# A gated scan and a cosine layer in one kernel: the queries' transposition, the squares of the logs, the split weights, the guards and the verdict change places

## The chip, the cores and the metric

The kernel runs on one core of a Trainium2 chip. The metric is the device time of one execution in microseconds (us). A core has TensorE (PE; its weight loads are listed as PEld), VectorE (DVE), ScalarE (ACT), GpSimd (POOL) and SyncE (SP). Each has an instruction queue of its own that runs in order; what stands behind a waiting instruction waits too. Transfers are issued by SP, POOL or ACT and carried out by 16 DMA engines that all of them share.

## What is computed

```python
# gateloop, q, k, v, a_re, a_im: (4, 8, 768, 48)
mag = np.sqrt(a_re * a_re + a_im * a_im)
scale = np.minimum(mag, 0.999) / (mag + 1e-06)
a_re_n, a_im_n = (a_re * scale, a_im * scale)
for t in range(S):
    new_re, new_im = ar * S_re - ai * S_im, ar * S_im + ai * S_re
    S_re, S_im = new_re + k_t v_t^T, new_im
    y[:, :, t] = q_t S_re
# act_gcu on x = y as (3072, 384); w_in (384, 2048), w_out (2048, 384)
h = x @ w_in
return ((h * np.cos(h)) @ w_out).astype(np.float32)
```

The weights arrive as doubles: the program reads them as 64-bit words and makes floats of them.

## The kernel before

**Groups and stages.** The 3072 rows are 24 chunks of 128 steps; two chunks make a group, so there are 12 groups. The recurrence is done in closed form: running sums of the logarithms of the decay (`lgs`, one matmul by a triangle of ones) and of its phase (`phs`), powers `P` and `Q` of them, then keys and queries multiplied by powers and by cosine and sine (`ks`, `qs`, made in `g_stack`), scores `sc` of chunk against chunk, masked into `atm`, and outputs `yp`. These go through DRAM into `xT`, the input of the cosine layer.

Groups 0 and 1 run in an order written out by hand. From group 2 on a loop `for n in range(2, NG)` builds one stage for each n. Stage n does, in this order on PE: the scores and outputs of group n (`chunks`) and, between them, the second product (`products`: `sum` and `op`) of group n-1; `lgs` and `phs` of group n+1; and the first product (`first`, tiles `hp`) of group n in eight parts `jp` of 256 columns. The scores of the next stage follow directly on the last `hp`.

**Who sets the order.** `weave` sorts the steps of a stage by the places given as fractions and emits them. PE's order is fixed by that (`chain`), as are the table functions of ACT (`special`, with the squares of the logs) and POOL's transfers. On DVE and the rest of ACT a planner orders the instructions when the program is built, by its own estimate of the times: of those that it takes to be ready, the one emitted first goes first. `behind(a, b)` makes it put a after b on the same engine, with no wait on the chip. SP and DVE run then in the order so found.

**Keys and queries.** `f_transpose` (lines 932 to 952) turns `ks` and then `qs` on DVE (tile `tr`), writes the result to DRAM (`moved`), and reads it back as `kT` (four transfers) and `qT` (one), all on SP. The turn of the queries of group n+1 stands behind `X[n]["gated"]`, the first gate product of group n.

**Gates.** For each jp, ACT computes the sine of `hp` (the cosine, by a shifted phase) into `gate` and the square of `hp` for the check of its range (`junk`); DVE multiplies (`gate<-hp,gate`). `hp` has three places in PSUM, so a jp can start when the gate three before it is done.

**Three halves.** For jp 4 to 7 and from a certain group on (`FROM`), the product is made of three products of rounded halves: of the weights (`wh`, `wl`, `wx`, made once by `three_halves`: three passes on DVE, two on ACT) and of x (`xh`, `xl`, `xx`, made in every group by `x_halves`). The crossed product `hb` comes out on ACT (`cross_out`) and is added on DVE (`whole_sum`, rows `hp<-hp,gate`) behind the gate product of the jp before, so for these jp sine, square, product and sum of two neighbours take turns.

**Logs.** `log_steps` starts with two squares on ACT (`lg<-re`, `tan<-im`) and their sum, then logarithms and exponentials (another table of ACT), and splits the sum's argument `lg` into `hi` (ACT) and `lo` (DVE) for PE. In before these squares are emitted at the beginning of a stage, behind the last gate of the stage before.

**Guards.** From stage 4 on, two 768 KB pieces of the original weights are read again in every stage by POOL (`raw`), cut on DVE and checked on ACT (`guard`). They wait on POOL for the last gate of the stage before (`wait_for`). `raw` has the same single buffer (`tr`) as the turned keys, and in before the halves of the weights had it too.

**The tail.** After the loop: the seven products of the last group, for which the gates are mixed on DVE (`mixed`: `s<-gate`; `mixed_again`: `gate<-gate`, `gate<-s,gate`), and the `verdict`, small reductions of the checks whose result chooses between this output and a general path.

Of the kernel before, what the change touches and what calls it, by code (L numbers as in the profile page):

```python
# [487 lines left out]
def fast_path(ctx, tc, q, k, v, a_re, a_im, moe_w_in, moe_w_out, out, least, odd, wide,  # L488
# [158 lines left out]
    def guard(src):  # L647

        _, e = fetched(src)
        vector.tensor_scalar(out=e, in0=e, scalar1=1, scalar2=21,  # L650
                             op0=ALU.logical_shift_left, op1=ALU.logical_shift_right)
        scalar.activation(out=e.bitcast(F32), in_=e, func=AF.Relu, scale=-1.0, bias=least_e_b,
                          accum_out=odd[:, ds(next(odds), 1)])
# [80 lines left out]
    def log_steps(g, i, n):  # L734
# [40 lines left out]
        vector.tensor_tensor(out=mag, in0=mag, in1=sq, op=ALU.mult)  # L775
        if lower:
            lower()
# [154 lines left out]
    def f_transpose(g, i, n, name):  # L932


        if i == 0:
            X[g][name] = ft.tile([D2, G * H, Q4, 32] if name == "kT" else [D2, Q4, G * H, 32], F32,
                                 tag=name, name=name, bufs=1)
        pool, tag = (ft, "tr") if name == "kT" else (gt, "pair")
        tr = pool.tile([C, NB, n * H, 32], F32, tag=tag, name="tr", bufs=1)
        turn = vector.transpose(out=tr, in_=X[g][name[0] + "s"][:, ds(i * H, n * H)].rearrange(  # L940
            "p x a d -> p x (a d)").rearrange("p x (r b) -> p b x r", b=NB))
        X[g][name + " turn"] = turn
        if name == "qT" and "gated" in X[g - 1]:
            behind(turn, X[g - 1]["gated"])
        moved = rows_d.tile([Q4, D2, n * H, 32], F32, tag="moved", name="moved", bufs=3)
        nc.sync.dma_start(out=moved.rearrange("q (r b) x j -> (q r) b x j", b=NB), in_=tr)
        if name == "kT":
            for q4 in range(Q4):
                nc.sync.dma_start(out=X[g][name][:, ds(i * H, n * H), q4], in_=moved[q4])
# [21 lines left out]
    def f_scores(n, hh):  # L971
# [5 lines left out]
        for h in range(HH):  # L977
# [4 lines left out]
            out=y["atm"][:, ts(hh, HH)], in0=ps, in1=causal.unsqueeze(1).to_broadcast([C, HH, C]), op=ALU.mult)  # L982

# [111 lines left out]
    def halves(g):  # L1095

        if g == PLAIN:
            for name in "wl", "wx":
                right[name] = stage["pool"].tile([C, len(THREE), ND, 256], F32R, name=name)
        for n, jp in enumerate(THREE):  # L1100
            if FROM[jp] == g:
                yield from three_halves(jp, right["wl"][:, n], right["wx"][:, n])

    def three_halves(jp, wl, wx):

        cut_ = ft.tile([C, ND, 256], F32, tag="tr", name="cut", bufs=1)
# [3 lines left out]
        yield  # L1110
        vector.tensor_tensor(out=wl, in0=w, in1=cut_, op=ALU.subtract)
        w_in[jp] = wts.tile([C, ND, 256], F32R, tag=f"w_in{jp}", name="wh", bufs=1)
        scalar.copy(out=w_in[jp], in_=cut_)
        yield
        vector.scalar_tensor_tensor(out=wx, in0=wl.bitcast(F32), scalar=-SHIFT, in1=cut_,
                                    op0=ALU.mult, op1=ALU.add)
        scalar.mul(out=wl, in_=wl.bitcast(F32), mul=SHIFT)

    def x_halves(g):
# [14 lines left out]
        def lower():  # L1134
            scalar.copy(out=x["xh"], in_=x["cut"])
            low = vector.tensor_tensor(out=x["xl"], in0=all_of(), in1=x["cut"], op=ALU.subtract)
            if g + 1 < NG:
                behind(low, X[g + 1]["qT turn"])

        def apart():  # L1140
            vector.scalar_tensor_tensor(out=x["xx"], in0=x["xl"].bitcast(F32), scalar=-SHIFT,
                                        in1=x["cut"], op0=ALU.mult, op1=ALU.add)
# [6 lines left out]
    def mm1_three(g, jp, ps):  # L1149
# [27 lines left out]
        for part in (straight, crossed) if k == 0 else (crossed, straight):  # L1177
            part()
# [8 lines left out]
    def whole_sum(g, jp):  # L1187
        ps = X[g]["hp"][jp]
        behind(vector.tensor_tensor(out=ps, in0=ps, in1=X[g]["gate"][jp], op=ALU.add),
               X[g]["product"])  # L1190

    def gate_sine(g, jp):
# [6 lines left out]
        scalar.activation(out=junk, in_=ps, func=AF.Square, scale=size,  # L1199
                          accum_out=wide[:, ds(g * (NJ // 2) + jp, 1)])  # L1200

    def gate_product(g, jp):
# [8 lines left out]
        x.setdefault("gated", gated)  # L1211
# [32 lines left out]
    FROM, UPPER, SHIFT = {4: 2, 5: 3, 6: 3, 7: 4}, 0xFFFFF000, 4096.0  # L1244
# [23 lines left out]
    def mixed(g, p):  # L1268
# [4 lines left out]
        vector.tensor_tensor(out=s1, in0=a21, in1=a22, op=ALU.add)  # L1273
# [73 lines left out]
    def stepwise(part, count):  # L1347

        part = iter(part)
        return [lambda: next(part, None) for _ in range(count)]  # L1350

# [57 lines left out]
    def first(g):  # L1409
        return [lambda jp=jp: mm1(g, jp) for jp in range(NJ // 2)]  # L1410
# [8 lines left out]
    def guarded(g, count):  # L1419
# [3 lines left out]
        for _ in range(min(count, len(guards))):  # L1423
            yield lambda: guard(guards.pop(0))
# [281 lines left out]
    for n in range(2, NG):  # L1706
        turned_keys, plain = list(keys(n + 1)), n == PLAIN
        split = x_halves(n)
        if n + 1 < NG:
# [7 lines left out]
              (stepwise(halves(n), 3 * list(FROM.values()).count(n)), 0.1, 0.5),  # L1717
# [4 lines left out]
              (mixes(n, 0, 2), 0.92, 1.0), (guarded(n - 1, per) if n > 3 else [], 0.1, 0.56))  # L1722
# [6 lines left out]
    weave((mixes(NG - 1, 2, 4), 0.0, 0.1), ([judged], 0.05, 0.15),  # L1729
# [95 lines left out]
```

## Time and profile before

| | |
|---|---|
| runs | 676.52, 671.46, 675.76 us; median 675.76 |
| profiled execution | 675.03 us, its span 673.2 us |
| PE busy | 635.2 us, 94% |
| DVE busy | 534.6 us, 79% |
| ACT busy | 433.5 us, 64% |
| POOL busy | 30.7 us, 5% |
| DMA | 94.95 MB, mean 141 GB/s |

The profile records one execution: for each instruction its start, its duration and what ended the idle time before it. The span runs from the first instruction to the last. A row of the timeline names the start, the duration, the engine, the line, the operation, its tiles as output<-inputs, and in brackets the idle time of the engine before it with what ended that. Most rows carry the line of a helper (L678 for DVE and ACT, L689 for PE), so the tiles' names tell them apart. PEclk is the share of TensorE's full clock that was granted.

### The profile page before, as it was taken

What the parts mean: (1) busy time and instruction counts of PE and PEld (TensorE: products, weight loads), DVE (VectorE), ACT (ScalarE), POOL (GpSimd) and SP (SyncE); (2) the same over time, 40 slices, a digit from 0 to 9 for tenths busy, and PEclk for the clock granted to TensorE, in tenths of its full rate; (3) what the DMA queues carried; (4) which work ended last, traced back from release to release, by engine and by line L of the source; (5) the groups of instructions that cost most, each with busy time, mean ns of one, the idle gap of its engine ahead of it and who ended that gap; (6) DMA issues with size and microseconds to landing.
All of it is one profiled execution on the core that took longest, in us unless ns stands there. A gap on an engine that the chain in (4) does not pass through costs nothing. (4 is left out here: it accounts for less than half of the span.)

```text
span 673.2 us, 11371 instructions
## 1 busy us (share of the span) xinstructions
PE 635.2 (94%) x4291; PEld 573.7 (85%) x4291; DVE 534.6 (79%) x867; ACT 433.5 (64%) x790; POOL 30.7 (5%) x53
## 2 busy tenths in 40 slices
PE   8999999998999999899889999989989999999996
PEld 5888777766899898889889989988989988999995
DVE  6999999887897797797678788788879779864371
ACT  7898786465675693694676587577577578553340
POOL 4011100000000000010000000000000000000000
PEclk9999999999999999999989999989999999999999
DMA  9967846437527638638626836745764763354001
GB/s 244 245 186 171 271 117 168 103 83 185 108 48 188 142 94 212 165 105 182 181 64 159 203 98 158 201 112 124 206 136 110 190 135 114 100 136 141 23 1 31
DMA packets 232924, 94.95 MB, mean 141 GB/s; under 512 B 208701, under 2 KB 221246, under 8 KB 232858
## 3 DMA queue, kind: packets, MB, share of 16 engines
q1 hardware_dynamic: 225320, 68.51, 44.2%
q0 software_dynamic: 5824, 25.50, 11.5%
q8 instruction: 36, 0.59, 0.4%
q10 hardware_dynamic: 1714, 0.11, 0.2%
q14 instruction: 30, 0.25, 0.1%
HBM read 69.28 MB, written 24.81 MB: 140 GB/s over the span
## 5 line engine op out<-in xcount | busy, mean ns | idle before, releaser
L689 PE MATMUL hp<-xT,w_in 128*128 128x256 f32 (+1 forms) x744 | 160.3, 373 | 4.4 <-DVE gate L678 2.4
L689 PEld LDWEIGHTS hp<-xT,w_in 128*128 128x128 f32 x744 | 137.1, 190 | 25.0 <-DMA xT<-x 2.9
L689 PE MATMUL op<-w_out,gate 128*128 128x192 f32 (+1 forms) x464 | 103.6, 373 | 0.8 <-DVE gate L678 0.8
L709 ACT ACTIVATE gate<-hp,half_pi_b 128x512 f32<-128x512 f32 x96 | 66.0, 687 | 54.0 <-PE hp L689 29.2
L689 PEld LDWEIGHTS op<-w_out,gate 128*128 128x128 f32 x464 | 78.5, 190 | 18.2 <-issue 2.2
L678 DVE TENSOR_TENSOR gate<-hp,gate 128x512 f32<-128x512 f32 x60 | 40.9, 685 | 31.5 <-ACT junk L678 31.3
L689 PE MATMUL sc<-qT,kT 96*128 96x128 f32 x384 | 50.7, 281 | 11.6 <-DMA qT<-moved 10.1
L689 PEld LDWEIGHTS sc<-qT,kT 96*128 96x128 f32 x384 | 48.3, 196 | 14.5 <-issue 9.7
L689 PE MATMUL sum<-w_out,gate 128*128 128x192 f32 x304 | 56.9, 337 | 0.0
L678 ACT ACTIVATE junk<-hp 128x512 bf16<-128x512 f32 x96 | 56.8, 592 | 0.0
L689 PEld LDWEIGHTS sum<-w_out,gate 128*128 128x128 f32 x304 | 51.1, 196 | 0.0
L678 DVE SCALAR_TENSOR_TENSOR gate<-hp,gate 128x512 f32<-128x512 f32 x36 | 24.8, 690 | 24.0 <-ACT junk L678 24.0
L678 ACT ACTIVATE ot<-sum 128x192 f32<-128x192 f32 x39 | 12.7, 327 | 46.7 <-PE sum L689 46.5
L689 PE MATMUL hp<-xh,wh 128*128 128x256 f32 x216 | 38.5, 287 | 1.5 <-DVE gate L678 1.5
L678 DVE TENSOR_TENSOR atm<-sc,causal 128x512 f32<-128x512 f32 x48 | 32.5, 685 | 7.3 <-PE sc L689 7.3
L689 PE MATMUL hp<-xl,wl 128*128 128x256 f32 x216 | 37.3, 281 | 0.0
L689 PEld LDWEIGHTS hp<-xh,wh 128*128 128x128 f32 x216 | 30.9, 189 | 4.5 <-DVE gate L678 4.4
L678 DVE TENSOR_TENSOR gate<-gate 128x256 f32<-128x256 f32 x80 | 32.7, 419 | 2.3 <-PE op L689 1.4
L689 PE MATMUL yp<-atm,v 128*48 128x128 f32 x352 | 33.5, 277 | 0.0
L678 DVE TENSOR_TENSOR hp<-hp,gate 128x512 f32<-128x512 f32 x36 | 24.9, 693 | 9.1 <-ACT gate L678 9.1
L705 ACT ACT_TABLE_LOAD x24 | 30.8, 1283 | 1.2 <-PEq L1809 0.7
L689 PEld LDWEIGHTS hp<-xl,wl 128*128 128x128 f32 x216 | 30.6, 188 | 0.0
(163 smaller groups left out, 1248.9 us busy)
## 6 DMA issues: line engine op xcount, KB each, us to landing
moved<-tr SPq DMA_DIRECT2D x20, 768.0 KB
raw<-in_moe_w_in_dram POOLq DMA_DIRECT2D x16, 768.0 KB, 5.2
raw<-in_moe_w_out_dram POOLq DMA_DIRECT2D x16, 768.0 KB, 4.7
kT<-moved SPq DMA_DIRECT2D x40, 192.0 KB
qT<-moved SPq DMA_DIRECT2D x10, 768.0 KB
k<-in_k_dram SPq DMA_DIRECT2D x24, 192.0 KB
q<-in_q_dram SPq DMA_DIRECT2D x24, 192.0 KB
v<-in_v_dram SPq DMA_DIRECT2D x24, 192.0 KB
```

The source lines that it names most:

```text
L678: ins = getattr(self.engine, op)(**kw)
L689: chain(nc.tensor.matmul(out, **kw), "tensor")
L705: chain(nc.scalar.preload_act_table_set(table))
L709: chain(nc.scalar.activation(func=func, **kw))
```

## The change

- The queries' turn is no longer put behind the first gate product of the group; the copy `xh` is put behind the square of the gate emitted last, and `xl` and `xx` behind its product.
- `mm1` gets a flag for the last jp of a group. At that place the first step of the logs of group g+2 (two squares, their sum) is emitted, ahead of the last gate's sine. The sum of halves waits with its gate as `held` instead of looking at jp - 1.
- In the logs, `lo` is made before the product `pair<-pair,tan` and not behind it.
- The masked scores are put behind the last sum of halves of the group before.
- `FROM` goes from {4: 2, 5: 3, 6: 3, 7: 4} to {4: 3, 5: 3, 6: 4, 7: 4}. The halves of the weights are made in stage 2 (jp 4, 5) and stage 3 (jp 6, 7), at places 0.7 and 0.76, when that group has used the plain weights: `first` takes these jp first. Their buffer is that of `yT`.
- The guards' places go from three between 0.1 and 0.56 to 0.1 (the wait), 0.22 (the first) and 0.93 (the second, whose cut on DVE is put behind the gate product of its place).
- In the tail the verdict's first part is emitted first, then all four mixes of the last group, put behind its last gate product; before, two of the four stood in the stage's end.

```diff
-    def guard(src):
+    def guard(src, other=None):
...
+        if other is not None:
+            behind(ins, other)
@@ log_steps
-        vector.tensor_tensor(out=mag, in0=mag, in1=sq, op=ALU.mult)
         if lower:
-            lower()
+            X[g]["low"] = lower()
+        product = vector.tensor_tensor(out=mag, in0=mag, in1=sq, op=ALU.mult)
+        if lower:
+            behind(product, X[g]["low"])
@@ f_transpose
-        if name == "qT" and "gated" in X[g - 1]:
-            behind(turn, X[g - 1]["gated"])
@@ f_scores
+        if "whole" in X[n // G - 1]:
+            behind(y["masked"], X[n // G - 1]["whole"])
@@ halves of one jp (was a generator in three steps)
-        cut_ = ft.tile([C, ND, 256], F32, tag="tr", name="cut", bufs=1)
+        cut_ = ft.tile([C, ND, 256], F32, tag="yT", name="cut", bufs=1)
@@ x_halves
-            scalar.copy(out=x["xh"], in_=x["cut"])
+            behind(scalar.copy(out=x["xh"], in_=x["cut"]), x["square"])
...
+            behind(low, x["product"])
...
+            behind(vector.scalar_tensor_tensor(
+                out=x["xx"], in0=x["xl"].bitcast(F32), scalar=-SHIFT,
+                in1=x["cut"], op0=ALU.mult, op1=ALU.add), x["product"])
@@ mm1
-    def mm1(g, jp):
+    def mm1(g, jp, last):
+
         mm1_sums(g, jp)
         if three(g, jp):
             cross_out(g, jp)
-            if three(g, jp - 1):
-                mm1_gate(g, jp - 1)
+            if "held" in X[g]:
+                mm1_gate(g, X[g]["held"])
+            X[g]["held"] = jp
             whole_sum(g, jp)
-        if not three(g, jp) or jp == NJ // 2 - 1 or not three(g, jp + 1):
+        else:
             mm1_gate(g, jp)
+        if last:
+            if g + 2 < NG:
+                X[g + 2]["steps"] = log_steps(g + 2, 0, G)
+                next(X[g + 2]["steps"])
+            if "held" in X[g]:
+                mm1_gate(g, X[g]["held"])
@@
-    FROM, UPPER, SHIFT = {4: 2, 5: 3, 6: 3, 7: 4}, 0xFFFFF000, 4096.0
+    FROM, UPPER, SHIFT = {4: 3, 5: 3, 6: 4, 7: 4}, 0xFFFFF000, 4096.0
@@ mixed
+        if g == NG - 1:
+            behind(first_, X[g]["product"])
@@ first
-        return [lambda jp=jp: mm1(g, jp) for jp in range(NJ // 2)]
+        late_ = [jp for jp in THREE if FROM[jp] == g + 1]
+        order = late_ + [jp for jp in range(NJ // 2) if jp not in late_]
+        return [lambda jp=jp: mm1(g, jp, jp == order[-1]) for jp in order]
@@ guarded
-            yield lambda: guard(guards.pop(0))
+            yield lambda: guard(guards.pop(0), X[g + 1].get("product"))
@@ the loop
-              (stepwise(halves(n), 3 * list(FROM.values()).count(n)), 0.1, 0.5),
+              (convert[0:1], 0.7, 0.7), (convert[1:2], 0.76, 0.76),
...
-              (mixes(n, 0, 2), 0.92, 1.0), (guarded(n - 1, per) if n > 3 else [], 0.1, 0.56))
+              (mixes(n, 0, 2 * (n < NG - 1)), 0.98 if convert else 0.92, 1.0), (guard_[0:1], 0.1, 0.1),
+              (guard_[1:2], 0.22, 0.22), (guard_[2:3], 0.93, 0.93))
@@ the tail
-    weave((mixes(NG - 1, 2, 4), 0.0, 0.1), ([judged], 0.05, 0.15),
+    weave(([judged], 0.0, 0.0), (mixes(NG - 1, 0, 4), 0.01, 0.1),
```

More of the change, by code (lines that the diff above doesn't have):

```diff
@@ L1707, in fast_path @@
         turned_keys, plain = list(keys(n + 1)), n == PLAIN
-        split = x_halves(n)
-        if n + 1 < NG:
+        split = x_halves(n) if any(three(n, jp) for jp in THREE) else ()
+        guard_ = list(guarded(n - 1, per)) if n > 3 else []
+        convert = [lambda jp=jp: halves(jp) for jp in THREE if FROM[jp] == n + 1]
+        if FROM[THREE[0]] <= n < NG - 1:
             X[n + 1]["upper"] = split[0]
```

38 lines of the change are left out of this document (14 added, 24 removed).

## The prediction

> **What bounds the kernel now.** The page's engine line first, then the list of who made PE wait, over the whole span, cut to the entries that matter here.
>
> ```profile
> PE 635.2 (94%) x4291; PEld 573.7 (85%) x4291; DVE 534.6 (79%) x867; ACT 433.5 (64%) x790; POOL 30.7 (5%) x53
> ```
> ```profile
> PE sc L689 <- DMA qT<-moved: 10.1, 5, 3.2
> PE lgs L689 <- DVE lo L678: 7.3, 8, 1.4
> PE hp L689 <- DVE gate L678: 4.0, 5, 1.4
> PE hp L689 <- DMA xT<-x: 2.0, 2, 1.6
> ...
> PE sc L689 <- issue: 1.3, 1, 1.3
> ```
> PE is the bound, in one fixed order, so an edit is worth what it takes from PE's work or from these waits (total, times, longest), 24.7 us. Two kinds come back in nearly every stage: scores on the queries' transfer (11.4 in six, with the 1.3 put down to "issue" at the same place) and log sums on their lower halves.
>
> Some waits cost again. Three windows of 24 or 25 matmuls, each from the scores that ended such a wait; the clock is the third number from the end:
>
> ```profile
> 338.10:342.95 4.85, 4.85 (x24) 4.85 (x25) 2.54 (x6) 3.84 (x6) 0.74 (x2) 0.65 0.00 0
> ...
> 443.63:448.45 4.82, 4.82 (x25) 4.82 (x25) 3.87 (x8) 3.46 (x6) 1.04 (x2) 0.65 0.01 3
> 497.37:500.53 3.16, 3.16 (x24) 3.16 (x25) 3.16 (x8) 2.06 (x5) 0.00 (x0) 1.00 0.03 5
> ```
> ```profile
> 443.63 1.13 PE L689 MATMUL sc<-qT,kT 96*128 96x128 f32 x8 [1.72 <-DMA qT<-moved]
> ```
> ```profile
> 497.37 1.13 PE L689 MATMUL sc<-qT,kT 96*128 96x128 f32 x8 [1.95 <-DMA qT<-moved]
> ```
> Granted clock 0.65 instead of 1.00 and 4.85 or 4.82 us instead of 3.16: 1.7 us lost, twice, 3.4 in all: after the wait of 3.2 and after 1.72, not after 1.95.
>
> Now the queries' chain in stage 8, whose first product starts at 476.11; times from there are called T. DVE, ACT and SP:
>
> ```profile
> 479.55 0.56 DVE L678 TENSOR_SCALAR cut<-xT 128x768 uint32<-128x768 uint32 x1
> 482.22 0.69 DVE L678 TENSOR_TENSOR gate<-hp,gate 128x512 f32<-128x512 f32 x1 [2.12 <-ACT junk L678]
> 482.83 2.26 DVE L678 STREAM_TRANSPOSE tr<-qs 128x1536 f32<-128x1536 f32 x1
> ```
> ```profile
> 480.19 0.83 ACT L678 CAST xh<-cut 128x768 fp32r<-128x768 f32 x1 [3.55 <-DVE cut L678]
> ```
> ```profile
> 485.12 0.33 SPq L946 DMA_DIRECT2D moved<-tr  x1
> 485.54 4.70 SPq L949 DMA_DIRECT2D kT<-moved  x4
> ```
> The queries turn from T 6.7 to 9.0 only because the first gate stands ahead of them, and that is late because ACT waits 3.55 us with the copy xh ahead of the gate's sine. SP issues in order, so the four kT transfers, ready before, wait for the queries' store too. What the DMA engines do meanwhile (the last two numbers, share and GB/s):
>
> ```profile
> 482.10:485.50 3.40, 3.40 (x18) 2.99 (x17) 3.28 (x3) 2.51 (x7) 0.00 (x0) 1.00 0.01 2
> 485.50:496.10 10.60, 9.92 (x78) 9.29 (x76) 7.60 (x14) 6.41 (x14) 0.00 (x0) 1.00 0.99 222
> ```
> After the keys' store 3.4 us of nothing, then 10.6 us at 0.99, and 1.3 more until PE starts at 497.37. From the queries' store on, the engines are full.
>
> **The change part by part.**
>
> *Queries turned behind the keys.* With the edge gone and xh behind the square, the queries' turn can follow the cut (479.55 and 0.56: T 4.0) and end near T 6.2; if the planner lets the first gate go first, now ready near T 4 as well (matmuls to T 2.6, then sine and square), near T 6.9. I take 6.2: the store leaves 2.8 us earlier. By itself that brings the scores from T 21.3 to 18.5, ahead of PE, which is there at 495.42 (497.37 less 1.95), T 19.3: all 11.4 us gone. The first gate comes no later than now.
>
> *The second guard.* At 0.93 it stands behind the turned keys in the one buffer tr, and nothing else on POOL holds it, the wait for the last gate being long past. So its fetch starts when the keys' store has landed, near T 6 to 7, together with the queries' store. First a row in which a fetch leaves as soon as that buffer is free, then the share of POOL's queue in the window of one fetch (501.0 to 506.1), then both queues in a window (14.0 to 19.5) where such fetches met SP's small packets:
>
> ```profile
> 511.55 0.72 POOL L631 DMA_DIRECT2D raw<-in_moe_w_out_dram  x1 [9.59 <-ACT raw L678]
> ```
> ```profile
> q0 software_dynamic: 144, 0.79, 43.9%
> ```
> ```profile
> q0 software_dynamic: 555, 2.07, 94.7%
> q1 hardware_dynamic: 435, 0.12, 9.1%
> ```
> 43.9% of 5.1 us is 2.24 us of all 16 engines. Where they met, POOL's queue kept 94.7% and SP's 9.1%. So the fetch goes through nearly unhindered, and the queries' chain loses between 0 (should the fetch fall into a hole) and 2.24 us; I take 2.2, the rows of the meeting being the nearest. Scores at T 20.7, PE's wait about 1.4, and this also at the end of stage 10, which has no wait now: 7 x 1.4 = 9.8 for 11.4, **-1.6**. Of six waits now two cost half the clock; of seven, each shorter than 1.72, I take one: **-1.7** of 3.4, between -3.4 (none) and +8.5 (all seven).
>
> The Trainium skill, "TensorE: Matmul & The Clock Gate", Part 1 (What's actually happening), lets the clock fall after an idle window of about 3.4 us. Here it fell after 1.72 us, so the rows decide; by the page none of the new waits would cost clock, and this term would be -3.4.
>
> *Squares ahead of the last sine, lo ahead of pair.*
>
> ```profile
> 498.47 0.69 ACT L709 ACTIVATE gate<-hp,half_pi_b 128x512 f32<-128x512 f32 x1 [1.43 <-DVE hp L678]
> ...
> 499.62 0.84 ACT L753 ACTIVATE lg<-re 128x768 f32<-128x768 f32 x1
> 500.35 0.84 ACT L753 ACTIVATE tan<-im 128x768 f32<-128x768 f32 x1
> ```
> ```profile
> 510.17 1.00 ACT L678 ACTIVATE raw<-raw,least_e_b 128x768 f32<-128x768 uint32 x1
> ```
> ```profile
> 509.62 0.95 DVE L678 TENSOR_TENSOR pair<-pair,tan 128x768 f32<-128x768 f32 x1
> 510.49 0.95 DVE L678 SCALAR_TENSOR_TENSOR lo<-lg,hi 128x768 fp32r<-128x768 f32 x1
> ```
> ```profile
> 511.50 0.45 PE L689 MATMUL lgs<-lo,exact 128*128 128x384 f32 x1 [0.96 <-DVE lo L678]
> ```
> ```profile
> PE lgs L689 <- DVE lo L678: 5.1, 6, 1.2
> ```
> The two squares, 0.73 us apart, fit into the 1.43 us that ACT waits ahead of the last sine; what follows on ACT comes 1.46 us earlier. lo gains 0.87 more (509.62 to 510.49). Against it stands the second guard's check, 1.0 us on ACT, now behind the gate of jp 5, where sines and sums take turns: if it falls between, the last sine is that much later. Net 1.3 to 2.3 us for a wait of 0.96, of which the shorter wait for queries, 0.55, takes back a part. The last row is the list of waits from 209 us on; of its 5.1 I leave 0.3: **-4.8**. Without the cover of the queries' wait PE would come 1.4 us sooner and wait here for what is missing. The two earlier waits, 7.3 less 5.1, lie in groups 2 and 4; lo moves by 0.87 in both, the squares in the second alone: **-1.6** of 2.2.
>
> *Guards and halves out of the second products.* In stage 4 now:
>
> ```profile
> 258.14 0.56 DVE L678 TENSOR_SCALAR raw<-raw 128x768 uint32<-128x768 uint32 x1 [2.10 <-DMA raw<-in_moe_w_in_dram]
> ```
> DVE stands 2.1 us for the second fetch, in the middle of the phases, and the fetch shares the engines with the transfer of xT: of the waits on xT the longest, **-1.6**, goes. Of the 4.0 for gates, all in stages 2 to 4, jp behind three halves are the longest; in stages 2 and 3 the plain jp now come first, but halves of 2.35 us each on DVE (0.56 and twice 0.95, less overlap) come among the gates. **-1.0**, between -4.0 and +2 for a gate held up by one such set.
>
> *FROM.* Two jp, one in stage 2 and one in stage 3, become plain again.
>
> ```profile
> 476.11 10.52 PE L689 MATMUL hp<-xT,w_in 128*128 128x256 f32 x48
> ...
> 489.55 0.51 PE L689 MATMUL hp<-xh,wh 128*128 128x256 f32 x3
> ...
> 491.69 0.52 PE L689 MATMUL hp<-xh,wh 128*128 128x256 f32 x3
> ```
> A plain jp takes 10.52 / 4 = 2.63 us; of three halves one starts 2.14 after the other. 2 x 0.49 = **+1.0**.
>
> *The tail.* All mixes of the last group now stand behind its last gate product.
>
> ```profile
> 650.67 1.10 DVE L678 TENSOR_TENSOR gate<-gate 128x256 f32<-128x256 f32 x3
> ...
> 652.02 0.68 DVE L678 SCALAR_TENSOR_TENSOR gate<-hp,gate 128x512 f32<-128x512 f32 x1
> 652.62 0.24 DVE L1762 TENSOR_REDUCE most<-wide 128x1 f32<-128x96 f32 x1
> ```
> ```profile
> 652.76 0.92 PE L689 MATMUL op<-w_out,gate 128*128 128x192 f32 x4 [0.82 <-DVE gate L678]
> 653.51 0.65 PE L689 MATMUL sum<-t_s,gate 128*128 128x192 f32 x3
> ```
> Without mixes ahead of it the last gate can come up to 0.4 us earlier (the mix ahead of it goes) and end at 652.2. Then come about 0.5 of verdict (the reduction and small ones) and, at 0.34 each (three took 1.10), four sums, four differences and the one that the third product reads first: 652.2 + 0.5 + 9 x 0.34 = 655.8, where PE now starts at 653.51. **+2.3**; +3.3 with the last guard's check in between, nothing if the planner still mixes earlier.
>
> Sum: -1.6 -1.7 -4.8 -1.6 -1.6 -1.0 +1.0 +2.3 = -9.0: the span goes from 673.2 to 664.2, and with the 1.8 us around it the execution from 675.03 to 666.0. The median of the runs, 675.76, is 0.7 above that execution: **667**.
>
> **The rivals.**
>
> *The fetch hides.* If it falls into holes of the chain, no score waits. For it: 482.10 to 485.50 shows the engines empty just there. Against it: with the turn moved that hole closes to under 1 us. Then the log sums bind: PE wants lo 1.95 us before 510.54, T 32.5; lo ends at 511.44 less 1.3 to 2.3, T 33.0 to 34.0. Per stage 1.4 is saved and 0.5 to 1.5 paid, say 0.5 seven times, and 1.7 of clock: **662**.
>
> *Each wait costs the clock.* If all seven waits of 1.4 bring the 1.7 us that 1.72 brought, 10.2 more: **677**, no change. For it 443.63, against it 497.37 and three more of the six.
>
> *The fetch in front, the turn not earlier: slower.* If the planner keeps the turn behind gates and it still ends at T 9.0, the fetch, issued at T 6 to 7, is wholly ahead of the queries' store: scores at T 23.5, a wait of 4.2, seven times 2.8 more than forecast, and the clock as after 3.2 us, six times 1.7 more: 667 + 19.6 + 10.2 = **697**. It decides from a turn that ends past about T 7.5, where 1.3 us in seven stages eat the gain. Against it: of what DVE has, only the first gate is ready about as early.
>
> **How the numbers follow.** The forecast (661 to 671) has 0.5, the hidden fetch (656 to 662) 0.17, the clock, or a gain given back in log sums or tail (671 to 677), 0.22, the slower case 0.11. The range, 656 to 677, holds all but the last and some edges. One per cent, 6.8 us, is about what a measurement of this kernel can tell from no change. Under 669 lie the hidden fetch and most of the forecast: 0.6; within one per cent 0.29; slower 0.11.
>
> **What would show it.** The queries' turn right behind the cut, near T 4; xh no longer ahead of the first sine; the second raw fetch at T 6 to 7, between the two stores, and sc <- qT near 1.4 in seven stages, the tenth included; lgs <- lo under 0.3; the squares ahead of the last sine; in the tail 2 to 3 us of PE ahead of sum<-t_s. The prediction is wrong if the scores' wait is gone or over 2 us, or if gates hold hp up for several us in stages 2 and 3.

## The result, and the profile after

The changed kernel takes 670.45 us (median of 20 runs, 665.73 to 676.51) where the kernel before takes 673.75 beside it (20 runs): a ratio of 0.9934, with a 95% interval of 0.9907 to 0.9961. The ratios of this document leave out the one run of the changed kernel that counts as slow (676.51) and are not the quotients of the medians. That is a gain of 0.4 to 0.9 per cent, within the one per cent that the prediction called no change, though the interval shuts out none at all. The profiled execution took 670.13 us, its span 668.2: 5.0 less than the 673.2 before, where the forecast had 9.0 less.

The engine line of the page, then the list of who made PE wait over the whole span (total, times, longest), of the changed kernel:

```profile
PE 634.7 (95%) x4279; PEld 575.4 (86%) x4279; DVE 528.7 (79%) x862; ACT 432.9 (65%) x787; POOL 31.2 (5%) x53
```
```profile
PE sc L691 <- DMA qT<-moved: 7.8, 6, 3.0
PE hp L691 <- DVE gate L680: 5.1, 1, 5.1
PE sum L691 <- DVE gate L680: 2.5, 1, 2.5
PE sc L691 <- issue: 2.5, 2, 2.3
PE lgs L691 <- DVE lo L680: 2.2, 3, 1.1
```

Scores on the queries' transfer now wait 10.3 us (7.8 and 2.5) for 11.4 before, log sums on their lower halves 2.2 for 7.3. The waits for gates were 4.0 us in five pieces; now they are one piece of 5.1, and the tail has a new one of 2.5. Where these two fall is seen in a table by stage. The first two rows are the kernel before (its stage 2, that is the third group's, and its last stage with the tail), the next two the same stretches of the changed kernel; the first number after the stretch is its length, the third from the end the granted clock:

```profile
155.49:209.06 53.57, 51.08 (x336) 46.91 (x337) 46.23 (x72) 34.88 (x63) 0.00 (x0) 1.00 0.52 118
...
628.11:673.16 45.05, 37.74 (x234) 35.73 (x232) 16.01 (x38) 13.94 (x33) 0.00 (x0) 0.97 0.06 16
```
```profile
155.78:213.24 57.46, 52.32 (x331) 48.13 (x331) 45.01 (x69) 34.75 (x62) 0.00 (x0) 0.97 0.49 112
...
620.54:668.17 47.63, 39.76 (x234) 37.40 (x232) 18.37 (x43) 15.65 (x36) 0.00 (x0) 0.96 0.05 15
```

Stage 2 became 3.9 us longer and the tail 2.6. The stages between them became shorter by 11.8 in all (from 209.06 to 628.11, 419.05 us, against 213.24 to 620.54, 407.30), each of them but stage 10, which became 0.5 longer. The start of stage 2 moved by 0.3. The terms of the prediction that fall between (scores, clock, log sums from 209 us on, xT) come to 9.7, and 2.2 us of waits for gates in stages 3 and 4 are gone beside them. So what was to gain there did gain; the part on gates, which was to gain 1.0, lost more in stage 2 than these 2.2.

What made stage 2 longer is on ACT and DVE, ahead of PE's wait of 5.14 us (three fences of the changed kernel's timeline: start, duration, and in brackets the idle time before and who ended it):

```profile
159.07 2.25 DVE L680 STREAM_TRANSPOSE tr<-ks 128x1536 f32<-128x1536 f32 x1
...
161.28 2.23 DVE L680 STREAM_TRANSPOSE tr<-qs 128x1536 f32<-128x1536 f32 x1
...
165.07 0.96 DVE L680 SCALAR_TENSOR_TENSOR wx<-wl,cut 128x768 fp32r<-128x768 f32 x1
168.16 0.69 DVE L680 TENSOR_TENSOR gate<-hp,gate 128x512 f32<-128x512 f32 x1 [2.12 <-ACT junk L680]
```
```profile
166.12 0.84 ACT L680 ACTIVATE wl<-wl 128x768 fp32r<-128x768 f32 x1 [8.83 <-DVE wx L680]
166.87 0.67 ACT L711 ACTIVATE gate<-hp,half_pi_b 128x512 f32<-128x512 f32 x1
```
```profile
168.90 0.71 PE L691 MATMUL hp<-xT,w_in 128*128 128x256 f32 x1 [5.14 <-DVE gate L680]
```

ACT stood 8.83 us with a pass over the weights' halves at the head of its order, waiting for wx, which DVE reached only behind both transposes of the next group. The first sine of the stage was behind it (an experiment below shows it ready at T 2.9, with T counted from the stage's first product). So the first gate's product came at 168.16, T 12.4, and PE, which had filled its places, waited for it. The clock fell with the wait:

```profile
168.90:172.90 4.00, 4.00 (x11) 3.23 (x12) 3.06 (x4) 3.38 (x7) 0.00 (x0) 0.57 1.04 222
```

At 0.57 over 4.00 us, some 1.7 us more are lost behind it.

Stage 8 of the changed kernel, with T counted from its first product at 469.27, shows the queries' chain in its new form. DVE, POOL, SP and PE:

```profile
472.55 2.25 DVE L680 STREAM_TRANSPOSE tr<-qs 128x1536 f32<-128x1536 f32 x1
474.72 0.52 DVE L680 TENSOR_SCALAR cut<-xT 128x768 uint32<-128x768 uint32 x1
```
```profile
476.36 0.72 POOL L631 DMA_DIRECT2D raw<-in_moe_w_out_dram  x1 [32.88 <-ACT xh L680]
```
```profile
475.84 8.64 SPq L951 DMA_DIRECT2D kT<-moved  x4
484.59 0.86 SPq L953 DMA_DIRECT2D qT<-moved  x1
```
```profile
491.38 0.35 PE L691 MATMUL sc<-qT,kT 96*128 96x128 f32 x1 [3.04 <-DMA qT<-moved]
```

The queries turn from T 3.3 to 5.5, ahead of the cut and of the first gate; they ended at T 9.0 before. The second guard's fetch leaves at T 7.1, as forecast. SP needs 8.64 us to issue the four kT transfers, 4.70 before, and qT goes out only at T 15.3, where it went out at T 14.2 before. In this stage the earlier turn has won nothing, and its scores wait longest, 3.04 us. In five of the seven stages from stage 4 on, kT takes 6.27 to 6.93 us, qT leaves at T 13.2 to 14.0, and a part of the gain is left.

### The profile page after: what moved, and what is told of

Same layout as the page of the kernel before. It is cut to its first block, busy times and chain, and to the rows that moved or that the text cites. A ratio compares the mean times of both kernels' runs of the same rounds, so it can differ in the third digit from the quotient of the medians.

```text
span 668.2 us, 11342 instructions
## 1 busy us (share of the span) xinstructions
PE 634.7 (95%) x4279; PEld 575.4 (86%) x4279; DVE 528.7 (79%) x862; ACT 432.9 (65%) x787; POOL 31.2 (5%) x53
## 3 DMA queue, kind: packets, MB, share of 16 engines
q0 software_dynamic: 5824, 25.50, 11.4%
## 4 chain that ended last, share of the span: by engine, by line
PE 70%; ACT 9%; DVE 8%; DMA 7%; issue 4%; SPq 1%; ACTq 0%; POOL 0%; POOLq 0%; DVEq 0%
PE hp L691 23%; PE op L691 14%; PE sum L691 14%; PE yp L691 5%; PE sc L691 4%; PE sp L691 3%; DMA qT<-moved 3%; PE phs L691 2%; PE hb L691 2%; ACT junk L680 2%; DVE hp L680 1%; ACT gate L711 1%; DMA xT<-x 1%; DVE gate L680 1%; PE lgs L691 1%
## 5 line engine op out<-in xcount | busy, mean ns | idle before, releaser
L691 PE MATMUL hp<-xT,w_in 128*128 128x256 f32 (+1 forms) x768 | 166.5, 376 | 7.1 <-DVE gate L680 5.1
L691 PEld LDWEIGHTS hp<-xT,w_in 128*128 128x128 f32 x768 | 143.0, 192 | 28.1 <-DVE gate L680 5.5
L680 DVE TENSOR_TENSOR gate<-hp,gate 128x512 f32<-128x512 f32 x62 | 42.5, 685 | 37.3 <-ACT junk L680 37.0
L691 PE MATMUL sum<-w_out,gate 128*128 128x192 f32 x304 | 54.6, 328 | 0.0
L691 PEld LDWEIGHTS sum<-w_out,gate 128*128 128x128 f32 x304 | 49.2, 190 | 0.0
L691 PE MATMUL hp<-xh,wh 128*128 128x256 f32 x204 | 37.0, 290 | 0.0
L691 PE MATMUL hp<-xl,wl 128*128 128x256 f32 x204 | 35.2, 281 | 0.0
L691 PE MATMUL sum<-t_s,gate 128*128 128x192 f32 x160 | 31.7, 352 | 2.5 <-DVE gate L680 2.5
L691 PEld LDWEIGHTS sum<-t_s,gate 128*128 128x128 f32 x160 | 27.4, 201 | 5.4 <-issue 4.4
L691 PE MATMUL yp<-qT,state 96*48 96x128 f32 x304 | 30.4, 278 | 0.0
```

Of the source, the lines that this page charges most:

```text
L680: ins = getattr(self.engine, op)(**kw)
L691: chain(nc.tensor.matmul(out, **kw), "tensor")
```

## The experiments

Each kernel of the table has its ratio to runs of the kernel before on the same chip.

| kernel | median us | ratio to before (95%) | profiled span |
|---|---|---|---|
| changed kernel | 670.45 | 0.9934 (0.9907 to 0.9961) | 668.2 |
| halves behind the gates | 662.39 | 0.9827 (0.9767 to 0.9887) | 662.9 |
| mixes early | 668.14 | 0.9915 (0.9883 to 0.9947) | 666.2 |
| second guard held back | 675.84 | 1.0049 (1.0020 to 1.0078) | 673.7 |
| turn behind the gate again | 682.95 | 1.0169 (1.0078 to 1.0260) | 682.9 |
| squares back | 693.16 | 1.0281 (1.0236 to 1.0326) | 692.4 |
| lo back | 667.06 | 0.9865 (0.9820 to 0.9911) | 669.2 |
| halves behind the gates, no second guard | 653.72 | 0.9704 (0.9666 to 0.9743) | 651.3 |
| halves behind the gates, mixes early | 660.97 | 0.9796 (0.9766 to 0.9825) | 659.6 |
| the same, guard among second products | 654.34 | 0.9692 (0.9652 to 0.9732) | 649.8 |
| before, log part alone | 665.44 | 0.9839 (0.9790 to 0.9889) | 663.8 |
| before, queries' part alone | 670.41 | 0.9951 (0.9909 to 0.9993) | 668.1 |

The kernel before took 674.14, 674.77 and 673.96 us in the three sets.

**Halves behind the gates.** The theory was that the place of the halves, and nothing else in the first gates, costs stage 2 its time.

```diff
 def halves(jp):
-    vector.tensor_scalar(out=cut_..., in0=w..., scalar1=UPPER, ...)
+    x = X[FROM[jp] - 1]
+    behind(vector.tensor_scalar(out=cut_..., in0=w..., scalar1=UPPER, ...), x["product"])
...
-    scalar.copy(out=w_in[jp], in_=cut_)
-    scalar.mul(out=wl, in_=wl.bitcast(F32), mul=SHIFT)
+    behind(scalar.copy(out=w_in[jp], in_=cut_), x["square"])
+    behind(scalar.mul(out=wl, in_=wl.bitcast(F32), mul=SHIFT), x["square"])
```

> The changed kernel with one edit: of each set of halves in the first halves of stages 2 and 3, the cut on VectorE comes behind the pair product and the two ScalarE passes behind the squared gate of the jp ahead of its own. Theory: in stage 2 ScalarE stood 8.83 us with the halves' copy ahead of the first sine, and so PE waited 5.14 us for a gate and then ran at 0.97 of the clock. Then that wait falls under 1.5 us, stage 2 goes from 57.5 to about 52, and the span from 668.2 to 661 to 664. Rival: the halves only take turns with the gates on VectorE, whatever the order; then the wait moves to a gate a jp later or to the products from halves, stage 2 stays above 56 and the span within 1 us of 668.2.

The median fell to 662.39, the profiled span to 662.9, and stage 2 to 50.63 us; in PE's list of waits hp waits for no gate any more. First ACT's first sine of stage 2 in this kernel, then the table's row of the stage:

```profile
158.05 0.69 ACT L711 ACTIVATE gate<-hp,half_pi_b 128x512 f32<-128x512 f32 x1 [1.89 <-PE hp L691]
```
```profile
155.16:205.79 50.63, 50.63 (x331) 47.01 (x332) 43.53 (x69) 34.30 (x61) 0.00 (x0) 1.00 0.56 127
```

The sine comes at T 2.9 of the stage, when PE has finished its input, where it came at T 11.1 (166.87). PE is busy for all of the 50.63 us at full clock. The stage shrank by 6.8; the span shrank by 5.3, because stages 4 and 9 grew by 2.5 and 1.9: their scores waited 3.1 and 2.1 us instead of 2.3 and 1.2, and both lost clock (0.97 over the stage, 1.00 in the changed kernel). The theory holds and the rival, a wait that only moves, does not. The edit puts one pass of DVE and two of ACT behind the gates; that ACT's order is what counted rests on the trace of the changed kernel, where DVE stood idle for 2.12 us ahead of the first gate's product, waiting for ACT.

**Mixes early.** This puts the tail back.

```diff
-        if g == NG - 1:
-            behind(first_, X[g]["product"])
...
-              (mixes(n, 0, 2 * (n < NG - 1)), 0.98 if convert else 0.92, 1.0), ...
+              (mixes(n, 0, 2), 0.98 if convert else 0.92, 1.0), ...
...
-    weave(([judged], 0.0, 0.0), (mixes(NG - 1, 0, 4), 0.01, 0.1),
+    weave((mixes(NG - 1, 2, 4), 0.0, 0.1), ([judged], 0.05, 0.15),
```

> The changed kernel with the last group's mixes as in the kernel before: its first sums and differences in stage 10 and the verdict among the rest. Theory: the mixes behind the last gate are the 2.48 us wait and the two of 0.82 and 0.41 us ahead of them at the end; then the waits of the tail fall from 3.7 to about 1 us and the last stretch goes from 47.6 to 45 us, the span from 668.2 to 665.5 to 666.5. Rival: what ends last there is the last gate or the guards' check, and the early mixes only hold up gates; then PE waits as much ahead of the third product, and the span stays within 0.5 us of 668.2.

The last stretch, 47.63 us in the changed kernel, is 45.87 here:

```profile
620.31:666.18 45.87, 37.83 (x234) 35.73 (x232) 18.42 (x43) 15.67 (x36) 0.00 (x0) 0.97 0.05 16
```

The span is 2.0 shorter and the median 2.3. The wait of 2.48 us ahead of the third product is gone from the list. The intervals of the two ratios overlap, so that the gain rests on this stretch of the profile. The two waits of op grew from 1.2 to 1.7 us in all, so the tail is not quite what it was.

**The second guard held back.** In stages 4 to 10 its fetch waits on its queue for the gate of jp 4, so that in stage 8 it leaves at T 16.8 and not at T 7.1.

```diff
+        hold = [lambda: wait_for(X[n]["gate"][4][0:1, 0, 0:1])] if 3 < n < NG - 1 else []
...
-              (guard_[1:2], 0.22, 0.22), (guard_[2:3], 0.93, 0.93))
+              (guard_[1:2], 0.22, 0.22), (hold, 0.925, 0.925), (guard_[2:3], 0.93, 0.93))
```

> The changed kernel with one edit: the second guard's fetch in the stages of groups 4 to 8 waits on its queue for the gate of jp 4, so that it starts some 10 us later, behind the queries' transfer. Theory: the fetch between the two stores is what is left of the scores' waits (10.3 us in eight places, 1.0 to 3.0 each); then those of the stages with a second guard fall from about 1.1 to under 0.4, and with them held away the log sums wait for their halves instead, 0.5 to 1 us per stage; the span falls by 2 to 5 us to 663 to 666. Rival: the queries' transfer is as late without the fetch, because the store, the four transfers behind it and the weights' streams fill the engines from the store on; then the scores' waits stay at about 1.1 per stage, and the span within 1 us of 668.2, or above it where the late check of the guard holds up a sine.

Neither the theory nor the rival came out whole. The scores' waits went, as the theory said: 0.4 us are left of 10.3. But the span rose by 5.5. In this kernel's list of waits stands what took their place, and on DVE the reason for a part of it:

```profile
PE yp L691 <- DVE atm L680: 6.0, 7, 1.5
PE lgs L691 <- DVE lo L680: 5.3, 6, 1.5
...
PE lgs L691 <- ACT hi L732: 4.1, 4, 1.9
```
```profile
493.40 0.56 DVE L680 TENSOR_SCALAR raw<-raw 128x768 uint32<-128x768 uint32 x1 [1.08 <-DMA raw<-in_moe_w_out_dram]
```

These three kinds take 15.4 us, 3.4 in the changed kernel. Behind the scores DVE stands 1.08 us for the late weights in the middle of gates and masks, and ACT's part of the check follows among the log steps. Summed over the list, PE's waits are hardly more than in the changed kernel (29.5 us for 29.0). Of the 5.5 of span, 5.1 are PE's own time, 639.8 us for 634.7, at a mean granted clock of 0.984 for 0.992; stage 9, with log-sum waits of 1.94 and 0.63 close together, has 0.94. Whether all of the 15.4 is the check, or PE's coming sooner would have brought it anyway, this kernel can't tell; the one without the second guard, below, does.

**The turn behind the gate again.** The edge that the change took away.

```diff
         X[g][name + " turn"] = turn
+        if name == "qT" and "gated" in X[g - 1]:
+            behind(turn, X[g - 1]["gated"])
...
+        x.setdefault("gated", gated)
         x["product"] = gated
```

> The changed kernel with the edge of the kernel before put back: the queries turn behind the first gated tile of the stage. Theory: the turn's place is what keeps the scores' waits at 1.1 us although a fetch was put in front; with the turn 1.5 to 3 us later the scores wait 2.5 to 4 us in each of the stages with a second guard, PE's clock falls to about 0.65 behind some of them, and the span rises to 678 to 692. Rival: the planner has the first gate early now, the turn comes only 0.7 us later or less, the scores wait under 2 us each, and the span stays under 673.

682.95 us, 12.5 more than the changed kernel. In stage 8, which starts at 476.56 here, the turn and the fetch, and the list of waits:

```profile
481.25 2.26 DVE L680 STREAM_TRANSPOSE tr<-qs 128x1536 f32<-128x1536 f32 x1
```
```profile
484.31 0.72 POOL L631 DMA_DIRECT2D raw<-in_moe_w_out_dram  x1 [32.50 <-DMA moved<-tr]
```
```profile
PE sc L691 <- DMA qT<-moved: 17.7, 6, 3.9
PE sc L691 <- issue: 5.3, 2, 4.4
```

The turn ends at T 7.0, not at 5.5, and the scores wait 23.0 us instead of 10.3. This is the slower rival of the prediction in kind and place; its price was 697, and a turn of T 7.0 gives a good part of it. The waits make up about half of the 14.7 us that the span grew; the rest is clock (0.978 for 0.992). The prediction let the change lose only from a turn past about T 7.5; here it is slower than the kernel before at T 7.0.

**Squares back, and lo back.** Two kernels take the two edits of the log sums back singly.

```diff
         if last:
-            if g + 2 < NG:
-                X[g + 2]["steps"] = log_steps(g + 2, 0, G)
-                next(X[g + 2]["steps"])
```

> The changed kernel with the first log step of the next group back in its place behind the last sine. Theory: the squares ahead of that sine are worth up to 1.46 us per stage of ScalarE, which is most of why log sums now wait 2.7 us and not 8.4; then log sums wait 0.7 to 1.2 us in six or seven stages again, 6 to 8 us in all, and the span rises by 3 to 6 to 671 to 674. Rival: lo ahead of the pair product alone does it, or the scores' wait covers it; then the log sums' waits stay under 4 us and the span within 1 us of 668.2.

The span rose by 24.2 and the median by 22.7, four to eight times the expectation. In stage 8 of this kernel, DVE and then ACT:

```profile
504.78 0.43 DVE L680 TENSOR_TENSOR gate<-s,gate 128x256 f32<-128x256 f32 x1 [3.86 <-PE sum L691]
506.06 0.43 DVE L680 TENSOR_TENSOR gate<-s,gate 128x256 f32<-128x256 f32 x1 [0.85 <-PE sum L691]
```
```profile
507.81 0.69 ACT L711 ACTIVATE gate<-hp,half_pi_b 128x512 f32<-128x512 f32 x1 [5.82 <-DVE hp L680]
```
```profile
PE lgs L691 <- ACT hi L732: 9.6, 5, 2.8
```

The planner, given another set of due times, put two mixes ahead of the last gates on DVE. They wait for sums that PE does behind the scores, so the last sine comes 5.8 us late and the whole log chain after it. So this run measures an order of DVE and not the squares; whether the squares' edit prevents that order or only happens to go with another is not shown. The run does not price the edit; the log part alone, below, does.

```diff
+        vector.tensor_tensor(out=mag, in0=mag, in1=sq, op=ALU.mult)
         if lower:
-            X[g]["low"] = lower()
-        product = vector.tensor_tensor(out=mag, in0=mag, in1=sq, op=ALU.mult)
-        if lower:
-            behind(product, X[g]["low"])
+            lower()
```

> The changed kernel with the pair product ahead of the lower halves again. Theory: lo is on the path of the log sums and comes 0.87 us later in each group; with 2.7 us of waits there now, these grow by up to 0.87 in each of some seven stages, 4 to 8 us in all, and the span rises by 2 to 6. Rival: the pair product that is then done sooner is itself waited for by what follows, or the planner puts lo as early by itself; then nothing over 1 us changes.

The span is 669.2, 1.0 more, the median 667.06, and the intervals of the two ratios overlap. The log sums' wait on lo is 1.0 us here, less than the 2.2 with lo ahead. The rival holds: within what these runs tell, no worth of lo's place is seen where the scores' wait stands ahead of it.

**No second guard.** On top of the halves behind the gates (662.9), the second guard is left out, fetch and check, in all eight stages that have one (the text put on record names groups 4 to 9, but eight fetches are gone); that part of the weights is not looked at.

```diff
-              (guard_[1:2], 0.22, 0.22), (guard_[2:3], 0.93, 0.93))
+              (guard_[1:2], 0.22, 0.22), ([lambda: guards.pop(0)] if guard_[2:3] else [], 0.93, 0.93))
```

> The kernel with the halves behind the gates (span 662.9) with the second guard of the stages of groups 4 to 9 left out, its fetch and its check: that part of the weights is not looked at. Theory: the fetch between the two stores is the whole of the scores' waits (8.2 and 3.3 us there), and holding it back cost 5.5 us because its check then stood among the softmax and the log steps; without both the scores' waits fall under 2 us in all, little comes in their place (log sums and yp under 3 us), and the span falls to 650 to 656. Rival: the scores' wait covers the other chains; without it PE comes 1 to 1.5 us sooner per stage to yp and to the log sums, and waits there instead, as in the kernel with the held fetch (15.4 us in these three); then the span stays between 660 and 668.

653.72 us, 8.7 less than with it, and the span 11.6 less. The list of waits:

```profile
PE lgs L691 <- DVE lo L680: 5.1, 5, 1.4
...
PE sc L691 <- issue: 1.7, 2, 0.9
```

The scores' waits fall from 11.5 us to 1.7; in their place the log sums wait 5.1 for 1.0. So the cover, what the scores' wait hid of the waits behind it, is about 4 us: PE comes sooner and meets the next late thing. The rest of the 15.4 us with the held guard goes with the guard itself, late as it was there. Both theories were right in part; the span is the first one's.

**Halves behind the gates, mixes early.** Both edits of above.

> The kernel with the halves behind the gates, and the last group's mixes as in the kernel before. If the two do not touch each other, the 5.3 us of span of the first edit and the 2.0 of the second add up: span 660 to 661.5, ratio to the kernel before 0.978 to 0.981. Rival: the mixes of stage 10 meet what the first edit moved (it left the scores' waits longer, 11.5 for 10.3 us), and the sum is short by over 1 us.

The span is 659.6, 3.3 less than with the halves alone (expected 2.0), the median 1.4 less. The interval of the ratio overlaps that of the halves alone, so the second gain is not clear of noise by itself; nothing here speaks against the two adding up.

**The guard among the second products.** On top of the last kernel, the second fetch goes back behind the first one, out of the queries' way, without a part left out.

```diff
-              (guard_[1:2], 0.22, 0.22), (guard_[2:3], 0.93, 0.93))
+              (guard_[1:2], 0.22, 0.22), (guard_[2:3], 0.48, 0.48))
```

> The kernel with the halves behind the gates and the early mixes (span 659.6), with the second guard's fetch back among the second products, behind the first guard's, where the kernel before has it. Theory: the fetch between the two stores is all that the guard costs; then the scores' waits go from 12.2 us to under 2.5, log sums go from 1.0 to about 5 as in the kernel without the guard, and the span falls to 650 to 654. Rival: among the second products its check holds up VectorE's phases or its fetch the transfer of xT, as in the kernel before (2.1 us of VectorE, 1.6 of PE in stage 4); if that recurs in each stage the queries come 1 to 2 us later again and the span stays above 657.

654.34 us, a ratio of 0.9692 (0.9652 to 0.9732): 16.1 us less than the changed kernel and the best full version of this study. The page's engine line, the list of waits, and SP in stage 8 (first product at 458.01):

```profile
PE 630.5 (97%) x4279; PEld 571.8 (88%) x4279; DVE 527.3 (81%) x862; ACT 432.6 (67%) x787; POOL 30.7 (5%) x53
```
```profile
PE lgs L691 <- DVE lo L680: 5.4, 7, 1.2
...
PE sc L691 <- issue: 0.4, 1, 0.4
```
```profile
465.45 4.55 SPq L951 DMA_DIRECT2D kT<-moved  x4
470.11 1.29 SPq L953 DMA_DIRECT2D qT<-moved  x1
```

kT takes 4.55 us to issue, not 8.64, and qT leaves at T 12.1, not T 15.3: these 3.2 us are what the fetch between the stores took from the queries in this stage. The scores' wait is gone but for 0.4. Of the rival's delays DVE has two, 2.23 and 2.90 us for the second piece in the first and the last stage with a guard, but PE waits there for neither phases nor xT.

**The parts alone.** Two kernels put one part each of the change into the kernel before: the squares with lo (as in the diffs above, turned round), and the queries' chain.

> The kernel before with two edits alone: the next group's first log step (the two squares) ahead of the last sine, and lo ahead of the pair product. Theory: the forecast's terms for the log sums, 4.8 and 1.6 us, are worth this where the scores' wait is as before; log sums go from 8.4 us of waits to under 2.5 and the span from 673.2 to 666 to 668.5. Rival: how much it is worth depends on the order that the planner gives VectorE (in the changed kernel, putting the squares back cost 24 us, because two mixes came ahead of the last gate); then the gain lies outside 4 to 8 us, or is a loss.

```profile
PE sc L689 <- DMA qT<-moved: 8.9, 6, 2.7
PE hp L689 <- DVE gate L678: 4.4, 8, 1.2
...
PE lgs L689 <- DVE lo L678: 1.4, 1, 1.4
```

The span fell by 9.4, the median by 8.5: more than the 6.4 of the forecast's two terms. The log sums' waits on lo went from 7.3 to 1.4, all of which lies ahead of stage 2; the scores wait 1.0 us less too. What else makes up the 9.4 was not taken apart.

```diff
-        if name == "qT" and "gated" in X[g - 1]:
-            behind(turn, X[g - 1]["gated"])
...
-            scalar.copy(out=x["xh"], in_=x["cut"])
+            behind(scalar.copy(out=x["xh"], in_=x["cut"]), x["square"])
...
+            behind(low, x["product"])
...
-            vector.scalar_tensor_tensor(out=x["xx"], ...)
+            behind(vector.scalar_tensor_tensor(out=x["xx"], ...), x["product"])
```

> The kernel before with the queries' chain alone changed: no edge from the queries' turn to the first gate, xh behind the square, xl and xx behind the gate's product; the guards, halves, logs and tail stay. Theory: by itself this takes all 11.4 us of the scores' waits; PE then comes 1.4 to 2 us sooner to the log sums in these stages, whose waits grow from 8.4 to 13 to 18, and the half clock (3.4 us) goes too: span 665 to 668. Rival: the turn moves but the transfers do not, because the engines are full from the store on; then the scores' waits stay over 7 us and the span within 2 us of 673.2.

```profile
PE lgs L689 <- DVE lo L678: 8.9, 8, 1.6
PE lgs L689 <- ACT hi L730: 6.5, 6, 1.8
...
PE sc L689 <- issue: 1.2, 1, 1.2
```

The scores' waits fall from 11.4 to 1.2, as the prediction said of this part by itself. But the log sums' rise from 7.6 (7.3 and 0.3) to 15.4, and only 5.1 of span (3.6 of the median) are left of the gain. Each part alone gains; of the queries' part three quarters of the saved waits go back to the next chain if that one is not shortened too. Two more things stand in this profile: no hp waits for a gate any more (4.0 us before), and the clock is lower, 0.984 in the mean of its ten runs for 0.992 in the 17 of the kernel before beside it.

## Why the prediction was right or wrong

The forecast was 667, the range 656 to 677, the measurement 670.45. Direction and range held, the gain was about half of what was forecast. That the time lies in the range doesn't confirm the sum: one term came out on the other side, and 1.3 of the 5.0 us come from waits that no term had. By the steps, in profiled spans:

- **Scores' waits, forecast 9.8 of 11.4: 10.3 measured.** Right, and for the reason given: the turn gives the scores back nearly all that the fetch takes. The part alone took 10.2 of 11.4 away, the fetch put about as much back, and without the fetch 1.7 are left. The place was right as well, T 7.1 for the fetch. The turn ended at T 5.5, ahead of the cut, where I had 6.2 behind it, but in the stage shown the queries' transfer left no sooner for that, since SP was held at kT. The waits are less even than forecast, 0.2 to 3.0 for 1.4 each, and two of them, 2.26 and 3.04, pass the 2 us that the prediction named as a sign of being wrong.
- **The clock, 1.7 of 3.4 lost again: the scores' waits cost none in this profile**, though one was 3.04 us. It was lost elsewhere: behind the gate of stage 2 (0.97 over the stage, 1.00 before), behind a log sums' wait of 1.09 in stage 7 (0.97 too) and in the tail (0.96 for 0.97). The mean is 0.992 for 0.993, so of the 1.7 nothing came. Over all runs it is worse: the 20 of the changed kernel have 0.982 to 0.994, 0.9885 in the mean, where the 47 of the kernel before in the three later sets have 0.9926. By these means the clock takes some 3 us from the median gain, which is an estimate.
- **Log sums, 6.4 to be gained: 5.1 on lo (7.3 to 2.2).** Right in kind; alone the part brought 9.4 of span. That the squares' edit carries it is likely, since lo's place moved nothing that can be told, but no run has the squares alone. That the shorter scores' wait "takes back a part" was right and underrated as a rule: the kernel with the queries' part alone shows the log sums paying 7.8 us for 10.2.
- **xT in stage 4, 1.6: gone** from that stage. The changed kernel's profile has one such wait of 1.9 in the part written out by hand, at 87.86, which no other profiled run here shows.
- **Gates, forecast -1.0: +1.1 of waits and 1.7 of clock. This is the step that failed.** The waits went from 4.0 to 5.1, all in one place, and the clock was lost behind it. The prediction bounded the term at +2, "for a gate held up by one such set", and sized the set by DVE's 2.35 us. The set does not only take turns on DVE: two of its passes stand in ACT's order, and one of them went ahead of the first sine while its input was behind two transposes of 2.25 and 2.23 us. The price is that chain, 8.83 us of ACT and 5.14 of PE, and the clock. With the set behind its gates the span fell 5.3 and the median 8.1 (the ratios' intervals, 0.9767 to 0.9887 and 0.9907 to 0.9961, do not meet). The prediction named "gates hold hp up for several us in stages 2 and 3" as what would make it wrong; it came in stage 2 alone. The old waits for gates did go, but the prediction put that to the plain jp going first: the queries' part alone, which leaves the order of jp as it was, has none of them.
- **FROM, +1.0:** not taken apart, nor is the masks' new place, which had no term. Stage 2 of the kernel with the halves behind the gates, which has one more plain jp, is still 2.9 us shorter than before, so what it costs is covered by what the gates gained there.
- **The tail, forecast +2.3: +2.6 measured**, and taking it back brought 2.0 of span and 2.3 of the median. Nine mixes at 0.34 after the last gate were the right count. The last gate's product started 24.4 us into the stretch, 23.9 before, and not 0.4 sooner.

The rival of the hidden fetch does not hold: its absence is worth 8.7 us. Its pricing of the log sums, 0.5 to 1.5 per stage without the cover, is what the kernels without it show: 0.4 to 1.2 in stages 4 to 9 of the best one.

One thing had no term. Ahead of the first product from halves the kernel before loses time that the list of PE's waits doesn't count, since it stands with the weight load of that product. Before, then after:

```profile
486.59 0.41 PEld L689 LDWEIGHTS hp<-xh,wh 128*128 128x128 f32 x3 [0.35 <-DVE gate L678]
```
```profile
479.41 0.52 PEld L691 LDWEIGHTS hp<-xh,wh 128*128 128x128 f32 x3
```

The load waits 0.34 or 0.35 us for a gate in six stages of the kernel before, and in none of the changed one. From the end of the last plain product to the next kind of product (`hp<-xl,wl`) it is 0.39 to 0.42 us in these stages before and 0.18 to 0.20 after; six times 0.21 are 1.3 of the 5.0. The kernel with the queries' part alone has no such wait either, so that part, with its earlier gates, is enough for it.

## What to carry to other kernels

A step that is moved into another stage has to be followed on every engine on which it has a pass: its place in the order of the engine that only copies can cost more than its work on the engine that computes. When a wait is removed, price the next chain behind it at the earlier time, since PE's wait was also that chain's cover. And a large fetch off the path is best put where neither its packets nor its check meet a chain that is due: against its place at T 7.1, the same fetch cost 5.5 us of span more at T 16.8 and 9.8 less among the second products.

## What the runs showed of the hardware

The granted clock does not follow from the length of a wait alone. Of the changed kernel the window behind the wait of 3.04 us quoted above, and of the kernel with the halves behind the gates a wait of 1.86 and the window behind it (the clock is the third number from the end):

```profile
491.38:494.38 3.00, 3.00 (x23) 3.00 (x24) 2.71 (x5) 2.98 (x6) 0.00 (x0) 1.00 0.02 5
```
```profile
432.35 0.35 PE L691 MATMUL sc<-qT,kT 96*128 96x128 f32 x1 [1.86 <-DMA qT<-moved]
```
```profile
432.35:435.35 3.00, 3.00 (x14) 3.00 (x15) 2.24 (x4) 3.00 (x8) 0.00 (x0) 0.60 0.02 5
```

Full clock after 3.04 us, 0.60 after 1.86. Of eighteen waits of the scores between 1.7 and 3.15 us in the thirteen profiles, eleven brought a lower clock (0.50 to 0.72 over the 3 us behind) and seven none; of the shorter ones none did, and the six longer ones all did. Short waits close together are another matter: two log-sum waits of 1.40 and 1.52 us, one behind the other in the kernel with the queries' part alone, brought 0.50. The Trainium skill, "TensorE: Matmul & The Clock Gate", Part 1 (What's actually happening), says that the activity window runs freely and does not start with the kernel, so that the point of the change to full clock depends on where in it the first matmul falls. For the fall the same section of the Trainium skill gives an idle window of about 3.4 us. The runs do not agree with that, as 1.86 us were enough; a window that runs freely would fit the scatter of the falls, but no run here shows that it is the cause. In this kernel a scores' wait of 1.7 to 3.15 us is best priced as a chance of some 1.7 us more, and not by a threshold.
